# Packing eight row flags into one word and rolling a skipped path into a loop

## The chip, the cores and the metric

The kernel runs on one core of a Trainium2 chip. The metric is the device time of one execution, in microseconds (us); the profile adds the span from the core's first to its last instruction.

## The reference

Three layers follow each other on 3,072 tokens of 384 numbers:

- linear attention with a decaying state: `state = alpha * state + k v^T`, `y = q state`, for 4 batches of 8 heads;
- a dense layer: `h = x @ w_in`, `x = (h * cos(h)) @ w_out`, with 2,048 hidden numbers;
- a mixture of 8 experts: each token goes to the one expert with the greatest logit, and gets `gate * sigmoid * (relu(x @ w1[e]) @ w2[e])`, with 1,024 hidden numbers per expert.

Which expert a token goes to is known only on the chip, while the program runs.

## The kernel before

TensorE (PE) does the matrix products, most of them in three parts (high and low halves of both operands). Attention and the dense layer are staged in six groups of four units, with an order of work written out by hand over slots `J`. In each group the tokens are routed: `route_logits`, `route_rank` and `route_rows` work out the row of each token in a DRAM tensor `xs`, and `route_send` scatters the rows with four indirect DMAs issued by GpSimd (POOL). `xs` has a region of `REG` rows for each expert. `base` holds the next free row of each region, `ebase` its first row.

After the last group's dense layer the kernel goes over to the experts. The first 256 rows (`EARLY`) of expert 0 were sent by earlier groups, and `first(j)` and `second(j)` work on them while the last group is routed. Then `begin(0)` loads the other 192 rows of expert 0 (`load_rows`), `rows_trans` turns them on PE, and the loop over the eight experts runs: `e_stage1` for eight blocks of hidden numbers (two PSUM banks in turn, `banks[0]` and `banks[1]`), then the second product for each tile of rows, then `e_out`, which scales on ScalarE (ACT) and scatters the rows to `out` by an indirect DMA of POOL. `load_expert` loads the next expert's weights and splits them in halves in small steps, on SyncE's (SP) DMA queue, ACT and VectorE (DVE).

An expert's region has a fixed part of `CAP` = 448 rows. Where an expert has at most `LOW` = 384 rows, PE takes a shorter branch (`by_rows`, a branch on a register of PE, lines 649 to 657). The eight flags for it are worked out on DVE as a row of eight words, `fewi`, and PE loads them into eight registers just ahead of the loop (line 1031). Just before the loop three banks are set to zero (line 1037), and PE's first product of the loop writes the first of them.

Rows beyond `CAP` go through a general path after the loop. All engines load one word, the largest count of extra tiles (`nov`, line 1088), and branch over the path when it is zero (line 1089); with these inputs it is zero. The path is written out eight times, one copy for each expert, each with a loop over tiles inside. Line 1216 is the program's end. In the stretch of the loop the order on PE, ACT, DVE and SP is that of the code (`manual_schedule`); POOL's order, and the code after the loop, are placed by the scheduler.

Of the kernel before, what the change touches and what calls it, by code (L numbers as in the profile page):

```python
# [8 lines left out]
F32 = mybir.dt.float32  # L9
F32R = mybir.dt.float32r  # L10
BF16 = mybir.dt.bfloat16
U32 = mybir.dt.uint32
I32 = mybir.dt.int32
ACTF = mybir.ActivationFunctionType
ALU = mybir.AluOpType
AX = mybir.AxisListType
PSUM = bass.MemoryType.PSUM
ENG = mybir.EngineType
# [10 lines left out]
E = 8  # L29
# [5 lines left out]
CAP = 448  # L35
LOW = 384
NOV = -(-(NT - CAP) // 128)
REG = CAP + 128 * NOV
# [12 lines left out]
CEB = CW8 + GU * E  # L51
CTOK = CEB + E
CROW = CTOK + NU
CCOL = CROW + 1


@with_exitstack
def kernel(
# [11 lines left out]
    nc = tc.nc  # L70
# [38 lines left out]
    base = const.tile([128, E], F32, name="base")  # L109
# [415 lines left out]
    def route_rows(g):  # L525
        oh, rp = rk.pop(g)
        t = s_p.tile([128, GU, E], F32, tag="rk", name="rk")
        nc.vector.tensor_tensor(
            out=t, in0=rp[:, 0], in1=base.rearrange("p (o e) -> p o e", o=1).to_broadcast([128, GU, E]), op=ALU.add
        )  # L530
        nc.vector.tensor_tensor(out=t, in0=t, in1=oh, op=ALU.mult)
        pf = s_p.tile([128, GU, 1], F32, tag="pf", name="pf")
        nc.vector.tensor_reduce(out=pf, in_=t, axis=AX.X, op=ALU.add)
        pu = s_p.tile([128, GU, 1], U32, tag="pu", name="pu")
        nc.vector.tensor_copy(pu, pf)
        nc.vector.tensor_tensor(out=base, in0=base, in1=rp[:, 1, 0], op=ALU.add)
        if g == NG - 2:

            nc.vector.tensor_scalar_max(base[:, 0:1], base[:, 0:1], float(EARLY))
        rk[g] = pu  # L540
# [404 lines left out]
    with tc.manual_schedule(engines={ENG.PE, ENG.Activation, ENG.DVE, ENG.SP}):  # L945
# [7 lines left out]
        def second(j):  # L953
            for t in range(n_t):
                e_part2(early, t, accs[t], j)
# [22 lines left out]
            x1_rows(g, s)  # L978
        route_rank(g)
        route_rows(g)  # L980
        for s in range(GU):
            route_send(g, s)
        second(1)
# [7 lines left out]
        second(5)  # L991
        first(7)
        second(6)
        m1.close()

        m2 = ExitStack()
# [5 lines left out]
        def begin(e):  # L1002
            r0 = EARLY if e == 0 else 0
            return load_rows(e, r0, CAP - r0, z_p, "xe")
# [4 lines left out]
        for t in range(n_t):  # L1009
# [2 lines left out]


        nt = o_p.tile([128, E + 1], F32, name="nt")
        few = o_p.tile([128, E], F32, name="few", bufs=1)
        fewi = o_p.tile([128, E], U32, name="fewi", bufs=1)
        nc.vector.tensor_tensor(out=nt[:, 0:E], in0=base, in1=ebase, op=ALU.subtract)
        nc.vector.tensor_scalar(
            out=nt[:, 0:E], in0=nt[:, 0:E], scalar1=float(127 - CAP), scalar2=127.0, op0=ALU.add, op1=ALU.max
        )  # L1020
        nc.vector.tensor_reduce(out=nt[:, E:E + 1], in_=nt[:, 0:E], axis=AX.X, op=ALU.max)

        nc.vector.tensor_scalar(
            out=few, in0=base, scalar1=float(LOW), scalar2=None, op0=ALU.subtract
        )
        nc.vector.tensor_tensor(out=few, in0=few, in1=ebase, op=ALU.is_le)
        nc.vector.tensor_copy(ntl, nt)
        nc.vector.tensor_scalar(out=ntl, in0=ntl, scalar1=7, scalar2=None, op0=ALU.logical_shift_right)

        nc.vector.tensor_copy(fewi, few)  # L1030
        few_r = nc.values_load_multi_w_load_instructions(fewi[0:1, 0:E], engines=[ENG.PE], min_val=0, max_val=1)[1]


        banks = [ps_h.tile([128, 512], F32, tag="h", name="hp") for _ in range(2)]
# [2 lines left out]
            nc.vector.memset(b, 0.0)  # L1037

        for e in range(E):
            r["few"], r["banks"] = few_r[e], banks  # L1040
            steps = load_expert(e + 1, vr_p if e % 2 else vl_p) if nxt else []

            def step():
                if steps:
                    for f in steps.pop(0):
                        f()

            hbs = []
            for j in range(NEF):

                n = r["n"]
                hb = h_p.tile([128, 2 * n], F32R, tag="hb", name="hb")
                e_stage1(r, j, hb[:, 0:n], [(slice(0, n - 64), hb[:, n + 64:]), (slice(n - 64, n), hb[:, n:n + 64])])
                hbs.append(hb)
                if j % 2:
                    step()
            r["gates"] = gates(z_p, r["xe"][:, :, DM:], len(r["tiles"]))
            n_t = len(r["tiles"])
            for i, t in enumerate((n_t - 1, *range(n_t - 1))):
                if i == n_t // 2 and nxt:  # L1060
                    rows_trans(nxt, z_p, "exh", "exl")
                step()
                if i == n_t - 1:
                    while steps:
                        step()
                ot = o_p.tile([128, DM], F32, tag="ot", name="ot")
                if r["tiles"][t] == 64:
                    op = e_acc(r, t, i, 128)
                    for m in by_rows(r.get("few"), (1, 0)):
                        if m:  # L1070
                            for j in range(NEF):
                                e_part2_both(r, t, op, j, hbs[j])
                    low = o_p.tile([64, DM], F32, tag="low", name="low", bufs=1)
                    nc.scalar.copy(low, op[64:128])
                    nc.vector.tensor_tensor(out=low, in0=op[0:64], in1=low, op=ALU.add)
                    op = low
                else:
                    op = e_acc(r, t, i)
                    for j in range(NEF):
                        e_part2(r, t, op, j)  # L1080
                e_out(r, t, op, ot)
            r = nxt
            nxt = begin(e + 2) if e + 2 < E else None
    m2.close()
    at2.close()


    nov = nc.values_load(ntl[0:1, E:E + 1], min_val=0, max_val=NOV)
    with tc.If(nov > 0):
        with tc.tile_pool(name="ov_p", bufs=1, side="left") as ov_p:  # L1090
            f1 = ov_p.tile([128, KD, EF], F32, name="f1")
            f2 = ov_p.tile([128, NEF, DM], F32, name="f2")
            rid = ov_p.tile([128, 1], F32, name="rid")
            lim = ov_p.tile([128, 1], F32, name="lim")
            far = ov_p.tile([128, 1], F32, name="far")
            ri = ov_p.tile([128, 1], U32, name="ri")
# [4 lines left out]
            oo = ov_p.tile([128, DM], F32, name="oo")  # L1101
            nc.vector.memset(zo, 0.0)
            nc.vector.memset(zo[:, ROW - 1:ROW], float(NT))
            for e in range(E):
                nc.sync.dma_start(out=f1, in_=w1[e].rearrange("(k p) f -> p k f", p=128))
                nc.sync.dma_start(out=f2, in_=w2[e].rearrange("(k p) f -> p k f", p=128))
                r0 = e * REG + CAP
                nc.vector.tensor_scalar_add(rid, c_sb[:, CROW:CROW + 1], float(r0))
                nc.vector.tensor_copy(lim, base[:, e:e + 1])
                n_e = nc.values_load(ntl[0:1, e:e + 1], min_val=0, max_val=NOV)  # L1110
                with tc.For_i(0, n_e, 1) as it:

                    nc.vector.tensor_tensor(out=far, in0=rid, in1=lim, op=ALU.is_lt)
                    nc.vector.scalar_tensor_tensor(
# [5 lines left out]
                        out=xs, out_offset=bass.IndirectOffsetOnAxis(ap=ri, axis=0),  # L1120
                        in_=zo, in_offset=None, bounds_check=E * REG - 1, oob_is_err=False,
                    )
                    nc.sync.dma_start(out=xo[:, 0, :], in_=xs[bass.ds(it * 128 + r0, 128), :])
                    gt, tk = gates(ov_p, xo[:, :, DM:], 1)
                    tp = ps_m.tile([128, KD, C], F32, tag="m", name="tp")
                    for k in range(KD):
# [28 lines left out]
def _layout(inputs):  # L1155
# [32 lines left out]
    for n in range(NU):  # L1188
        c[:, CTOK + n] = (n % B) * S + (n // B) * C + perm
    c[:, CROW] = np.arange(128)  # L1190
    return {
        "units": u.reshape(NU, 128, UCOL),
        "cst": c,
# [26 lines left out]
```

## Time and profile before

| | |
|---|---|
| device time, median of 3 runs | 814.5 us (813.9 to 815.12) |
| device time of the profiled execution | 812.32 us |
| its span | 810.5 us |
| mean granted TensorE clock | 0.981 |
| PE busy | 769.4 us (95%) |
| DVE busy | 501.9 us (62%) |
| ACT busy | 425.3 us (52%) |
| POOL busy | 316.6 us (39%) |

The device time of the profiled execution holds the span and 1.8 us around it. Busy times are those of instructions that do work: register loads, branches and semaphore instructions are not in them, and have rows of their own under the engine's name with a q (POOLq, PEldq).

### The profile page before, as it was taken

The page shows a single profiled execution, that of the slowest core. Times are in us where ns is not written, and L with a number is a line of the kernel's source. Part 1 is how long each engine was busy: PE and PEld are TensorE (multiplying, and loading weights), DVE is VectorE, ACT ScalarE, POOL GpSimd, SP SyncE. Part 2 cuts the span into 40 slices and gives each one's busy share as a digit, 9 for nine tenths or more (in the row PEclk, how much of TensorE's full clock was granted, in tenths as well). Part 3 has the DMA queues.
Part 4 walks back from the last instruction along what each step waited for, and adds up shares of the span by engine and source line. Part 5 has one row for each costly group of instructions (what it writes and reads, how often), then busy time and mean ns, then how long its engine had stood idle before and what let it go on. Part 6 is the DMA issues. An engine that isn't in the chain of part 4 may idle for free.

```text
span 810.5 us, 13963 instructions
## 1 busy us (share of the span) xinstructions
PE 769.4 (95%) x5346; PEld 655.7 (81%) x5346; DVE 501.9 (62%) x955; ACT 425.3 (52%) x782; POOL 316.6 (39%) x304
## 2 busy tenths in 40 slices
PE   8679899999999999999999999999699999999994
PEld 5557777888888888888888888889699999999994
DVE  8999998675467537663676334744565655655530
ACT  2454565754575457644665467555354545554420
POOL 3566756544355335543464424662011101101101
PEclk9998999999999999999999999999899999999998
DMA  9524452713201230113010101211565445645201
GB/s 326 205 94 159 170 199 100 243 60 112 80 1 54 73 125 1 54 59 109 31 55 20 41 0 59 89 50 44 182 192 181 135 142 176 191 123 159 67 13 34
DMA packets 46881, 85.31 MB, mean 105 GB/s; under 512 B 4152, under 2 KB 38488, under 8 KB 44240
## 3 DMA queue, kind: packets, MB, share of 16 engines
q1 hardware_dynamic: 43344, 74.67, 28.1%
q0 software_dynamic: 3456, 9.57, 3.2%
q8 instruction: 50, 0.82, 0.4%
q14 instruction: 31, 0.25, 0.1%
HBM read 69.01 MB, written 15.99 MB: 105 GB/s over the span
## 4 chain that ended last, share of the span: by engine, by line
PE 52%; issue 27%; DVE 11%; POOL 4%; DMA 2%; ACT 1%; POOLq 0%; SPq 0%; ACTq 0%; DVEq 0%
PE acc L418 22%; PE hp L379 21%; POOL out_dram L711 4%; DVE cv L347 3%; PE sc L211 2%; DMA un<-in_units_dram 2%; DVE cv L352 2%; PE yp L269 2%; PE yp L261 2%; DVE cv L356 2%; PE pp L285 1%; PE tp L442 1%; DVE t L397 1%; DVE t L392 1%; DVE w L151 1%
## 5 line engine op out<-in xcount | busy, mean ns | idle before, releaser
L405 POOL TENSOR_TENSOR gl<-t,gh 128x512 fp32r<-128x512 f32 x95 | 127.8, 1345 | 182.2 <-ACT gh L404 152.5
L386 ACT ACTIVATE t<-hp 128x512 f32<-128x512 f32 x96 | 57.3, 596 | 140.1 <-PE hp L379 130.4
L397 DVE TENSOR_TENSOR t<-hp,t 128x512 f32<-128x512 f32 x96 | 65.7, 684 | 89.3 <-ACT t L394 89.3
L392 DVE SCALAR_TENSOR_TENSOR t<-t,hp 128x512 f32<-128x512 f32 x96 | 65.7, 684 | 79.7 <-ACT t L386 79.6
L711 POOL DMA_INDIRECT out_dram<-ot,tk x32 | 31.3, 979 | 205.9 <-ACT ot L710 205.6
L687 PE MATMUL op<-h,hb 128*128 128x384 f32 x384 | 102.4, 338 | 1.7 <-PEq L654 1.7
L418 PE MATMUL acc<-gh,woh 128*128 128x512 f32 x288 | 90.3, 421 | 0.0
L677 DVE SCALAR_TENSOR_TENSOR hb<-hp,hb 128x64 fp32r<-128x64 f32 (+3 forms) x136 | 45.3, 372 | 70.1 <-ACT hb L675 70.0
L379 PE MATMUL hp<-xh,wih 128*128 128x512 f32 x288 | 83.6, 398 | 3.7 <-DVE t L397 3.1
L418 PE MATMUL acc<-gl,woh 128*128 128x512 f32 x288 | 84.2, 399 | 0.0
L418 PE MATMUL acc<-gh,wol 128*128 128x512 f32 x288 | 83.9, 399 | 0.0
L379 PE MATMUL hp<-xh,wil 128*128 128x512 f32 x288 | 82.6, 395 | 0.0
L379 PE MATMUL hp<-xl,wih 128*128 128x512 f32 x288 | 82.5, 395 | 0.0
L393 ACT ACTIVATE t<-t 128x512 f32<-128x512 f32 x96 | 60.7, 632 | 38.3 <-DVE t L392 38.3
L675 ACT ACTIVATE hb<-hp 128x448 fp32r<-128x448 f32 (+2 forms) x72 | 36.3, 504 | 72.3 <-PE hp L671 70.3
L599 DVE TENSOR_TENSOR l<-raw,h 128x768 fp32r<-128x768 f32 x60 | 57.3, 957 | 25.8 <-ACT h L595 25.0
L687 PEld LDWEIGHTS op<-h,hb 128*128 128x128 f32 x384 | 69.7, 188 | 3.0 <-issue 3.0
L394 ACT ACTIVATE t<-t,halfpi 128x512 f32<-128x512 f32 x96 | 69.6, 725 | 3.1
L379 PEld LDWEIGHTS hp<-xh,wih 128*128 128x128 f32 x288 | 54.4, 191 | 18.0 <-DVE t L397 2.2
L418 PEld LDWEIGHTS acc<-gh,wol 128*128 128x128 f32 x288 | 55.1, 191 | 13.4
L418 PEld LDWEIGHTS acc<-gl,woh 128*128 128x128 f32 x288 | 54.9, 191 | 12.8
L379 PEld LDWEIGHTS hp<-xl,wih 128*128 128x128 f32 x288 | 54.5, 189 | 12.9
(144 smaller groups left out, 1454.4 us busy)
## 6 DMA issues: line engine op xcount, KB each, us to landing
raw<-in_w_dram SPq DMA_DIRECT2D x64, 384.0 KB, 3.4
un<-in_units_dram SPq DMA_DIRECT2D x20, 1032.0 KB, 4.9
raw<-in_w_in_dram SPq DMA_DIRECT2D x16, 384.0 KB, 3.7
raw<-in_w_out_dram SPq DMA_DIRECT2D x16, 384.0 KB, 4.1
xs<-zrow SPq DMA_DIRECT2D x8, 591.0 KB, 5.8
xe<-xs SPq DMA_DIRECT2D x7, 591.0 KB, 5.1
un<-in_units_dram SPq DMA_DIRECT2D x4, 512.0 KB, 6.2
un<-in_units_dram SPq DMA_DIRECT2D x4, 256.0 KB, 6.8
```

The source lines that it names most:

```text
L379: nc.tensor.matmul(out=hp, lhsT=w[:, k, fs], rhs=x[:, k, :], start=(n == 0), stop=(n == 3 * KD - 1))
L386: nc.scalar.activation(out=t, in_=hps[g, j], func=ACTF.Copy, bias=MAGIC)
L392: nc.vector.scalar_tensor_tensor(out=t, in0=t, scalar=MAGIC, in1=hp, op0=ALU.subtract, op1=ALU.subtract)
L393: nc.scalar.activation(out=t, in_=t, func=ACTF.Abs)
L394: nc.scalar.activation(out=t, in_=t, func=ACTF.Sin, scale=-TWO_PI, bias=halfpi)
L397: nc.vector.tensor_tensor(out=t, in0=hps.pop((g, j)), in1=t, op=ALU.mult)
L405: eng.tensor_tensor(out=gl, in0=gf, in1=gh.bitcast(F32), op=ALU.subtract)
L418: nc.tensor.matmul(out=acc[g][k], lhsT=w[:, j, ks], rhs=a, start=(j == 0 and n == 0), stop=(j == NF - 1 and n == 2),)
L599: (nc.vector.tensor_tensor if i < 4 else sub)(out=lo, in0=raws[i], in1=h.bitcast(F32), op=ALU.subtract)
L677: nc.vector.scalar_tensor_tensor(out=out_, in0=hp[:, c], scalar=0.0, in1=hh[:, c].bitcast(F32), op0=ALU.max, op1=ALU.subtract)
L687: nc.tensor.matmul(out=op, lhsT=a[:, sl], rhs=w[:, j, :], start=(j == 0 and i == 0), stop=(j == NEF - 1 and i == 2))
L711: sent = nc.gpsimd.indirect_dma_start(out=out, out_offset=bass.IndirectOffsetOnAxis(ap=tk[0:n, t, :], axis=0), in_=ot[0:n], in_offset=None ...
```

## The change

- The constants get 16 more columns, of which eight hold the powers of two.
- Right after `route_rows` of the last group, DVE works out the eight flags, multiplies them by the powers of two, adds them up and casts the sum to one word, `fews`. The three DVE instructions that made `fewi` go.
- PE loads that one word after `second(6)`, and takes each expert's flag out of it by a shift and a mask at the head of that expert's turn.
- `nov` is loaded by all engines at the end of the turn of expert 6 and no longer after the loop.
- The general path is one loop over the experts with the loop over tiles inside, and so stands in the program once.

```diff
 CROW = CTOK + NU
-CCOL = CROW + 1
+CPW = CROW + 1
+CCOL = CPW + 16
...
         route_rank(g)
         route_rows(g)
+
+        cnt = s_p.tile([128, E], F32, tag="rk", name="cnt")
+        nc.vector.tensor_tensor(out=cnt, in0=base, in1=ebase, op=ALU.subtract)
+        nc.vector.scalar_tensor_tensor(
+            out=cnt, in0=cnt, scalar=float(LOW), in1=c_sb[:, CPW:CPW + E], op0=ALU.is_le, op1=ALU.mult
+        )
+        bits = s_p.tile([128, 1], F32, tag="pf", name="bits")
+        nc.vector.tensor_reduce(out=bits, in_=cnt, axis=AX.X, op=ALU.add)
+        fews = s_p.tile([128, 1], U32, tag="pu", name="fews")
+        nc.vector.tensor_copy(fews, bits)
         for s in range(GU):
             route_send(g, s)
         second(1)
...
         first(7)
         second(6)
+        few = nc.values_load(fews[0:1, 0:1], engines=[ENG.PE], min_val=0, max_val=(1 << E) - 1)
         m1.close()
...
         nt = o_p.tile([128, E + 1], F32, name="nt")
-        few = o_p.tile([128, E], F32, name="few", bufs=1)
-        fewi = o_p.tile([128, E], U32, name="fewi", bufs=1)
...
-        nc.vector.tensor_scalar(
-            out=few, in0=base, scalar1=float(LOW), scalar2=None, op0=ALU.subtract
-        )
-        nc.vector.tensor_tensor(out=few, in0=few, in1=ebase, op=ALU.is_le)
         nc.vector.tensor_copy(ntl, nt)
         nc.vector.tensor_scalar(out=ntl, in0=ntl, scalar1=7, scalar2=None, op0=ALU.logical_shift_right)
-
-        nc.vector.tensor_copy(fewi, few)
-        few_r = nc.values_load_multi_w_load_instructions(fewi[0:1, 0:E], engines=[ENG.PE], min_val=0, max_val=1)[1]
...
         for e in range(E):
-            r["few"], r["banks"] = few_r[e], banks
+            r["few"], r["banks"] = nc.tensor.snap((few >> e) & 1), banks
...
             r = nxt
             nxt = begin(e + 2) if e + 2 < E else None
+            if e == E - 2:
+                nov = nc.values_load(ntl[0:1, E:E + 1], min_val=0, max_val=NOV)
...
-    nov = nc.values_load(ntl[0:1, E:E + 1], min_val=0, max_val=NOV)
-    with tc.If(nov > 0):
+    with tc.If(nov > 0, label="ov"):
...
-            for e in range(E):
-                nc.sync.dma_start(out=f1, in_=w1[e].rearrange("(k p) f -> p k f", p=128))
-                nc.sync.dma_start(out=f2, in_=w2[e].rearrange("(k p) f -> p k f", p=128))
-                r0 = e * REG + CAP
-                nc.vector.tensor_scalar_add(rid, c_sb[:, CROW:CROW + 1], float(r0))
-                nc.vector.tensor_copy(lim, base[:, e:e + 1])
-                n_e = nc.values_load(ntl[0:1, e:e + 1], min_val=0, max_val=NOV)
-                with tc.For_i(0, n_e, 1) as it:
+            nc.vector.tensor_scalar_add(rs, c_sb[:, CROW:CROW + 1], float(CAP))
+            nc.vector.tensor_copy(ends_, base)
+
+            with tc.For_i(0, E, 1) as e:
+                nc.sync.dma_start(out=f1, in_=w1[bass.ds(e, 1)].rearrange("o (k p) f -> p (o k) f", p=128))
+                nc.sync.dma_start(out=f2, in_=w2[bass.ds(e, 1)].rearrange("o (k p) f -> p (o k) f", p=128))
+                nc.vector.tensor_copy(rid, rs)
+                nc.vector.tensor_scalar_add(rs, rs, float(REG))
+                nc.vector.tensor_copy(lim, ends_[:, 0:1])
+                nc.vector.tensor_copy(next_, ends_)
+                nc.vector.tensor_copy(ends_[:, 0:E - 1], next_[:, 1:E])
+                with tc.For_i(0, nov, 1) as it:
...
-                    nc.sync.dma_start(out=xo[:, 0, :], in_=xs[bass.ds(it * 128 + r0, 128), :])
+                    nc.sync.dma_start(out=xo[:, 0, :], in_=xs[bass.ds(it * 128 + e * REG + CAP, 128), :])
```

## Rows read from the trace of the kernel before

**Rows 1.** Stretches: busy us (count) of PE, PEld, DVE, ACT, POOL; granted clock; DMA share; GB/s.

```profile
570.71:576.10 5.39, 0.00 (x0) 0.03 (x1) 2.93 (x12) 0.61 (x2) 1.99 (x2) 0.91 0.98 308
576.10:581.94 5.84, 5.84 (x27) 5.84 (x28) 1.44 (x5) 1.38 (x3) 0.00 (x0) 0.50 0.17 66
581.95:588.00 6.05, 5.68 (x48) 5.44 (x48) 4.20 (x13) 3.14 (x8) 0.00 (x0) 1.00 0.42 130
```

**Rows 2.** Line 1031, PE's load of the flags: ns min/median/max, first and last start.

```profile
L1031 PEldq FUSED_REGOPS  x8: 146/146/160, 573.4 to 575.4; - x8
...
L1031 PEldq TENSOR_LOAD <-fewi x1: 788/788/788, 572.5 to 572.5; - x1
```

**Rows 3.** DVE in order of time, ahead of the expert loop: start us, busy us.

```profile
571.40 0.16 DVE L1021 TENSOR_REDUCE nt<-nt 128x1 f32<-128x8 f32 x1
571.48 0.16 DVE L1023 TENSOR_SCALAR few<-base 128x8 f32<-128x8 f32 x1
...
571.76 0.30 DVE L1027 CAST ntl<-nt 128x9 uint32<-128x9 f32 x1
572.09 0.17 DVE L1028 TENSOR_SCALAR ntl<-ntl 128x9 uint32<-128x9 uint32 x1
572.17 0.16 DVE L1030 CAST fewi<-few 128x8 uint32<-128x8 f32 x1
572.44 1.03 DVE L1037 MEMSET hp<- 128x512 f32 x2
```

**Rows 4.** PE and POOL in order of time, the last work of each.

```profile
798.85 0.34 PE L687 MATMUL op<-h,hb 128*128 128x384 f32 x1
...
800.13 0.98 POOL L711 DMA_INDIRECT out_dram<-ot,tk  x1 [3.18 <-ACT ot L710]
```

**Rows 5.** Line 1088, the load of the count, on PE and POOL.

```profile
L1088 PEldq TENSOR_LOAD <-ntl x1: 332/332/332, 795.9 to 795.9; - x1
...
L1088 POOLq TENSOR_LOAD <-ntl x1: 484/484/484, 799.9 to 799.9; - x1
```

**Rows 6.** Line 1089, the branch over the general path, on POOL.

```profile
L1089 POOLq EVENT_SEMAPHORE  x5: 17/43/43, 803.3 to 803.7; - x5
...
L1089 POOLq COMPARE_BRANCH  x1: 53/53/53, 800.4 to 800.4; - x1
...
L1089 POOLq INC_SWDGE_SEM  x1: 1286/1286/1286, 803.8 to 803.8; - x1
```

**Rows 7.** Line 1216, the program's end, on POOL.

```profile
L1216 POOLq DRAIN  x3: 40/107/4647, 805.1 to 810.3; - x3
```

**Rows 8.** PE in order of time, first product of expert 0.

```profile
583.10 0.55 PE L671 MATMUL hp<-exh,h 128*128 128x192 f32 x3
...
584.15 0.51 PE L671 MATMUL hp<-exh,h 128*128 128x192 f32 x3
```

**Rows 9.** Stretches around two earlier stalls of PE, columns as in rows 1.

```profile
88.99:90.42 1.43, 0.00 (x0) 0.02 (x1) 1.39 (x5) 1.43 (x4) 1.22 (x2) 1.00 0.30 53
90.46:93.87 3.41, 3.41 (x17) 2.83 (x18) 3.41 (x7) 1.74 (x4) 3.03 (x4) 1.00 1.03 397
135.16:136.95 1.79, 0.00 (x0) 0.00 (x0) 1.70 (x3) 0.62 (x2) 0.03 (x1) 1.00 0.00 0
138.26:141.65 3.39, 3.39 (x10) 2.61 (x9) 2.09 (x4) 2.31 (x5) 2.70 (x6) 0.50 0.66 210
```

**Rows 10.** One of PE's waits from 540 us on: total, times, longest.

```profile
PE hp L671 <- ACT hb L675: 0.4, 1, 0.4
```

**Rows 11.** DVE's first work after the last group's routing.

```profile
561.20 0.42 DVE L677 SCALAR_TENSOR_TENSOR hb<-hp,hb 128x256 fp32r<-128x256 f32 x1 [2.79 <-ACT hb L675]
```

**Rows 12.** Line 654, the branches on the flags, on PE.

```profile
L654 PEldq COMPARE_BRANCH  x108: 65/174/337, 575.7 to 781.8; - x108
```

**Rows 13.** DMA issues: count, KB each, us from issue to landing.

```profile
c_sb<-in_cst_dram SPq DMA_DIRECT2D x1, 160.5 KB, 4.4
```

**Rows 14.** Line 711 from 799.9 us: the last scatter, from issue to landing.

```profile
DMA to landing us min/median/max: 3.0/3.0/3.0
```

More of the change, by code (lines that the diff above doesn't have):

```diff
@@ L1093 @@
             rid = ov_p.tile([128, 1], F32, name="rid")
+            rs = ov_p.tile([128, 1], F32, name="rs")
+            ends_ = ov_p.tile([128, E], F32, name="ends_")
+            next_ = ov_p.tile([128, E], F32, name="next_")
             lim = ov_p.tile([128, 1], F32, name="lim")
@@ L1190, in _layout @@
     c[:, CROW] = np.arange(128)
+    c[:, CPW:CPW + E] = 2.0 ** np.arange(E)
     return {
```

## Prediction

> **What bounds the kernel now.** I read the busy shares first, then the stretches where PE is idle, then what ended each idle time, and last the records of line numbers that do no work of their own (loads of registers, branches), because the change is made of those. PE bounds nearly everything: once expert 0 is running it does 5.68 of 6.05 us [rows 1], and every other engine has slack beside it. A change to the other engines is worth only what it gives PE, or what it takes from the tail after PE's last product. Two places have such time.
>
> [...] In the idle time stand PE's load of the flags, 0.79 us at 572.5, and eight register operations from 573.4 to 575.4 [rows 2]. They can't begin before the flags' cast on DVE ends at 572.17 + 0.16 = 572.33 [rows 3].
>
> The second is the tail. PE's last product ends at 798.85 + 0.34 = 799.19 [rows 4], and the span ends at 810.5: 11.3 us in which POOL sends the last scatter [rows 4], loads the count [rows 5], takes the branch over the general path [rows 6] and drains [rows 7].
>
> **The stall ahead of the loop.** With the flags already in a register, the loads and register operations leave the gap. PE then waits for the next late thing: the zeroing of the first bank. Two memsets took 1.03 us from 572.44 [rows 3], 0.515 each, so the first bank is ready at 572.95 now. The three DVE instructions for `fewi` stood in front of it. Without them the cast to `ntl` follows the reduce, at the 0.20 us that dependent small instructions need here, at 571.60 instead of 571.76; the shift comes 0.33 later, as now, at 571.93; it takes 0.17, and with a gap of some 0.08 the memset starts at 572.18, 0.26 earlier. The bank is zero at 572.7, and with 0.1 us for the signal PE starts at 572.8. It starts at 576.10 now: **-3.3 us**. The stall is 2.1 us, no longer 5.4.
>
> **The half clock after it.** PE did 27 products in 5.84 us at 0.50 [rows 1]. At full clock nine take 584.15 - 583.10 = 1.05 us [rows 8], so 27 take 3.15: the half clock costs 2.7 us. Does a stall of 2.1 us still lead to it? One of 1.79 us at 135.16 was followed by 3.39 us at 0.50; one of 1.43 us at 88.99 was followed by full clock [rows 9]. 2.1 us is on the far side of both, so I take a half-clock stretch again, but a short one, 3.4 us as in that row rather than 5.8. By the same rates it costs 3.4 x (1 - 1.05/1.95) = 1.6 us. The difference is **-1.1 us**. The ends: nothing gained, if the stretch is as long as before, and 2.7 - 0.4 = 2.3 gained if there is none, where 0.4 is one more wait of the kind in [rows 10], the bank's eviction behind the split of the next weights, which the half clock hides now.
>
> All PE time saved here reaches the end, since PE has no other idle time of that size behind it, and expert 1's rows and weights are first needed when the whole of expert 0 is done.
>
> **What is added there.** Four small DVE instructions after `route_rows`, about 0.2 us apart by [rows 3]: 0.8 us. DVE is idle for 2.79 us right there [rows 11], so they cost nothing as long as POOL's four row scatters, which stand behind them in the code, wait only for the row numbers made before them. If they waited for the flags too, everything up to the loop would be 0.8 later. PE's load of one word is issued behind `second(6)`. The load of the count shows how that goes: it ran on PE's queue at 795.9 while products went on until 799.19 [rows 4, 5], so the queue is read 3.3 us ahead and a load of 0.33 to 0.79 us [rows 2, 5] hides in that. Its ends are 0 and 0.8; I take 0, by the nearer row, which is the same kind of load in the same position behind products. A shift and a mask for each expert are one or two register operations of 0.15 us [rows 2] ahead of that expert's first branch. The 108 branches of 0.07 to 0.34 us already hide in the lead [rows 12]; I take 0, the upper end is 8 x 0.3 = 2.4. The first block of constants grows by 16 columns of 128 rows, 8 KB on 160.5 KB with a landing time of 4.4 us [rows 13]: at most 0.2, taken as 0. The loads of `nov` on SP, DVE, ACT and PE move under expert 7's products, where each has slack of microseconds: 0.
>
> **The tail.** POOL's load of the count, 0.48 us at 799.9, goes, so its branch stands at 799.9 and not at 800.4 [rows 5, 6]. What then? The branch itself took 0.05 us, but POOL's next instruction came at 803.3: 2.85 us with nothing [rows 6]. The short branches of line 654, over some twenty instructions, take 0.07 to 0.34 us in all [rows 12]. So the distance matters, and now one copy of the path is jumped over instead of eight; I take the wait as gone. [...]
>
> Next is a wait for the scatters. The branch not taken raises the counters of the DMAs that the path would have issued. Today the path holds sixteen scatters in its eight copies, spread over all the scatter counters, so POOL waits for each of them, the last scatter's too, before it raises them (1.29 us at 803.8 [rows 6]). With two scatters in the one copy it should wait for fewer and older ones. The last scatter lands at 800.13 + 3.0 = 803.1 [rows 4, 14]; if POOL must still wait for it, only 0.5 us of the tail can go. If not, POOL's next limit is its own work on that scatter, until 801.1 [rows 4]. Then 1.29 us for the counters, a drain of 4.65 us [rows 7] and the same last 0.8 us give 801.1 + 1.29 + 4.65 + 0.8 = 807.9 instead of 810.5: **-2.6 us**. The ends are 0, if the drain waits for something that does not move, and 2.6.
>
> **Sum.** -3.3 - 1.1 - 2.6 = -7.0. The profiled execution took 812.3 us (its span and 1.8 around it), so the like execution would take 805.3. The median of the runs is 814.5, 2.2 above it; I carry the difference over: **807.5**.
>
> **The rivals.** (a) The tail moves little: the branch still waits 2.85 us, or POOL still waits for the last scatter, or the drain ends where it did. Then 0.5 us of it goes: 814.5 - 3.3 - 1.1 - 0.5 = 809.6. For it: the landing at 803.1 is only 0.7 us before the counters are raised. Against it: two scatters in the path instead of sixteen. (b) No half clock, with the tail as forecast: 814.5 - 3.3 - 2.3 - 2.6 = 806.3. For it: the full clock after 1.43 us; against: the half clock after 1.79. (c) One of the hidden pieces isn't hidden, the scatters wait for the flags or PE's load stands bare, and the tail gives 0.5: 809.6 + 0.8 = 810.4, or 811.5 with half the per-expert register work bare. (d) Slower: PE's load of `nov` behind expert 6 stops PE as the load of line 1031 does now, because it waits for DVE with nothing queued. Its price is the whole of today's stall, 5.4 + 2.7 = 8.1 us, and it decides from 7.0: 815.6. For it, PE's stall at 1031 is such a load; against it, the same word's load ran ahead of PE without a wait. (e) The change does nothing that counts: PE's gain is eaten by expert 1's weights and the tail stays, 814.5 or less by under 1.6. Nothing in the rows speaks for it.
>
> **How the numbers follow.** Forecast 0.42, (a) 0.30, (b) 0.14, (c) 0.08, (d) 0.04, (e) 0.02. The range reaches from a little under (b), with the tail and clock terms a little better than taken, to between (c)'s two values: 805.5 to 811.0. It holds the forecast, (a), (b) and half of (c). About 0.2% (1.6 us) can be told from no change here. Faster by more: all but (d), (e) and the bad edge of (c), 0.93; the same 0.03; slower 0.04.
>
> **What would show it.** Right: PE idle near 2 us before expert 0's first product, ended by the memset; no group of register operations in it; at most some 3.4 us at 0.50 after it; four DVE rows near 558.5 in idle time; POOL's first instruction after the branch within some 0.2 us of it, and the span ending less than 9 us after PE's last product. Wrong: a gap of PE at an expert's start, POOL's scatters of rows starting 0.8 us later, a wait of near 3 us behind POOL's branch, or a drain that is longer by as much as it starts earlier.

## The result, and the profile after

The changed kernel takes **805.39 us** (median of 4 runs, 803.29 to 807.06), the kernel before 814.71 us on the same chip (813.9 to 815.12): 9.3 us less, a ratio of 0.9886 with a 95% interval of 0.986 to 0.9911. The forecast was 807.5 us, a gain of 7.0, and its range ended at 805.5, 0.1 us above the result. The direction and the two places named were right; the size was too small, and a third place was missing. The profiled execution of the changed kernel took 805.95 us, its span 804.2.

The sections of the execution can be laid side by side, with the borders read as PE's starts and ends, in us:

| | before | after | difference | forecast |
|---|---|---|---|---|
| from the start to PE's last product ahead of the stall | 570.70 | 572.40 | +1.70 | 0 |
| PE's stall ahead of expert 0 | 5.40 | 2.32 | -3.1 | -3.3 |
| expert 0 | 19.93 | 18.80 | -1.1 | -1.1 |
| experts 1 to 7 | 203.15 | 202.10 | -1.05 | 0 |
| from PE's last product to the end | 11.35 | 8.57 | -2.8 | -2.6 |

These sum to -6.3, and the two profiled executions differ by 6.4 (812.32 and 805.95). I don't put the first line down to the change: up to there the work is the same but for the flags and the longer constants, and stretches of half clock fall differently from one execution to the next (mean granted clock from 26 to 144 us: 0.93 before, 0.90 after). In the profiles of the experiments below PE reached that point at 571.72 to 572.44 us without the flags' edit and at 571.02 to 572.95 with it; some tenths of a microsecond of cost can't be excluded by that. Without that line the change gains 8.0.

**The stall.** Stretches of the changed kernel, to set against [rows 1]; columns as there.

```profile
572.40:574.70 2.30, 0.00 (x0) 0.02 (x1) 1.99 (x8) 0.61 (x2) 1.62 (x2) 1.00 0.97 254
...
576.24:579.66 3.42, 3.42 (x19) 3.42 (x18) 1.80 (x5) 1.50 (x4) 0.00 (x0) 0.50 0.65 241
579.66:585.50 5.84, 5.47 (x46) 5.22 (x46) 3.85 (x12) 2.89 (x8) 0.00 (x0) 1.00 0.49 135
```

PE idles for 2.3 us in place of 5.4, and 3.42 us at 0.50 follow in place of 5.84. What ends the idle time stands in PE's waits from 572 us on:

```profile
PE hp L672 <- DVE hp L1039: 2.3, 1, 2.3
```

That is the zeroing of the first bank, as forecast, and DVE in order of time shows how it comes so late, beside [rows 3]:

```profile
573.32 0.45 DVE L1032 CAST ntl<-nt 128x9 uint32<-128x9 f32 x1
573.80 0.17 DVE L1033 TENSOR_SCALAR ntl<-ntl 128x9 uint32<-128x9 uint32 x1
574.08 1.02 DVE L1039 MEMSET hp<- 128x512 f32 x2
```

The three instructions for `fewi` are gone from between them. The cast takes 0.45 us here and 0.30 in [rows 3], which is most of the 0.2 us by which the stall is longer than the 2.1 forecast.

**The flags.** They are worked out on DVE right behind the last group's rows, first and last of the four:

```profile
559.90 0.17 DVE L984 TENSOR_TENSOR cnt<-base,c_sb 128x8 f32<-128x8 f32 x1
...
560.50 0.15 DVE L991 CAST fews<-bits 128x1 uint32<-128x1 f32 x1
```

Line 1005 is PE's load of the word, and line 655 the branches on its bits:

```profile
L1005 PEldq TENSOR_LOAD <-fews x1: 484/484/484, 567.4 to 567.4; - x1
L1005 PEldq FUSED_REGOPS  x1: 165/165/165, 568.0 to 568.0; - x1
```

```profile
L655 PEldq ALU_OP  x135: 36/36/42, 570.7 to 778.3; - x135
L655 PEldq COMPARE_BRANCH  x108: 67/174/345, 570.8 to 778.4; - x108
```

The load stands 5 us ahead of PE's stall and stops nothing. The shifts and masks came out as 135 register operations of 36 ns ahead of the 108 branches, more in number than the one or two for each expert that the prediction expected and shorter than its 0.15 us. PE waited on those branches in four places, 0.5 us at the longest and 1.8 us in all; before, by the same view of the waits, it was 0.4 us and 1.7 us, in four places too.

The view of POOL's waits names the flags as what the first scatter of rows waited for. Before and after:

```profile
559.12 0.99 POOL L544 DMA_INDIRECT xs<-xr,pu  x1 [6.50 <-DVE base L536]
```

```profile
560.58 0.99 POOL L545 DMA_INDIRECT xs<-xr,pu  x1 [6.51 <-DVE bits L989]
```

But the scatter starts as long behind the start of the sum into `base`, the last instruction of `route_rows`, as it did: 559.12 - 558.26 = 0.86 us before, 560.58 - 559.71 = 0.87 after, and 0.84 to 0.87 in the other eleven profiles. So the flags don't hold it up.

**The tail.** Loads of the count (line 1087), POOL's last scatter, the branch (line 1092) and POOL's drain (line 1227), beside [rows 4 to 7]:

```profile
L1087 PEldq TENSOR_LOAD <-ntl x1: 316/316/316, 762.5 to 762.5; - x1
...
L1087 POOLq TENSOR_LOAD <-ntl x1: 493/493/493, 796.3 to 796.3; - x1
```

```profile
796.56 0.98 POOL L712 DMA_INDIRECT out_dram<-ot,tk  x1 [3.18 <-ACTq L1092]
```

```profile
L1092 PEldq COMPARE_BRANCH  x1: 320/320/320, 792.4 to 792.4; - x1
...
L1092 POOLq COMPARE_BRANCH  x1: 45/45/45, 796.9 to 796.9; - x1
L1092 POOLq EVENT_SEMAPHORE  x1: 17/17/17, 797.4 to 797.4; - x1
L1092 POOLq INC_SWDGE_SEM  x1: 1278/1278/1278, 797.4 to 797.4; - x1
```

```profile
L1227 POOLq DRAIN  x3: 45/107/4638, 798.7 to 803.9; - x3
```

POOL's load of the count did not move: it still stands behind the last scatter's issue. But the next instruction after the branch comes 0.4 us later in place of 2.85, one wait of 17 ns stands there in place of five, and the raising of the counters (`INC_SWDGE_SEM`) starts at 797.4, before POOL's own work on the last scatter ends at 796.56 + 0.98 = 797.54 and before its landing at 796.56 + 2.8 = 799.4. In the records of the two traces the five waits and the raising name the semaphores of the last eight scatters, 111 to 118, the last one's (118) among them; the one wait and the raising in the changed kernel name 112 and 111 alone, those of the first two of the eight. The drain is as long as before and starts earlier. Counted from PE's end, the time behind the branch gives 2.4 us and the waits ahead of the counters 0.35; the rest of the tail is as long as before.

Is that time the jump, or a wait for the last scatter, which landed at 803.1, just ahead of POOL's next instruction at 803.3? DVE, whose branch comes 12 us before that scatter is issued, settles it. Before and after:

```profile
L1089 DVEq EVENT_SEMAPHORE  x2: 21/21/21, 790.8 to 790.9; - x2
...
L1089 DVEq COMPARE_BRANCH  x1: 63/63/63, 787.9 to 787.9; - x1
```

```profile
L1092 DVEq COMPARE_BRANCH  x1: 63/63/63, 783.7 to 783.7; - x1
L1092 DVEq EVENT_SEMAPHORE  x1: 21/21/21, 784.3 to 784.3; - x1
```

It too lost 2.8 us before and 0.5 after, with that scatter not yet issued. So the time goes with the length of the jump. The DMA queues of the kernel before, from POOL's branch to its next instruction (800.4 to 803.3 us), show packets of the kind `instruction` (count, MB, share of 16 engines):

```profile
q8 instruction: 1, 0.02, 2.2%
q14 instruction: 2, 0.02, 1.9%
```

The same view of the kernel after, from 796.9 to 797.4, has none. That these packets make the 2.85 us, or a part of it, isn't shown by this.

**Experts 1 to 7.** Stretches of the changed kernel, experts 1 and 6 and 7, and then the same three of the kernel before:

```profile
593.51:624.78 31.27, 31.27 (x174) 30.05 (x174) 18.24 (x37) 14.81 (x27) 4.25 (x4) 1.00 0.58 176
...
734.61:765.61 31.00, 31.00 (x173) 30.07 (x173) 15.96 (x33) 14.52 (x26) 3.87 (x4) 1.00 0.27 82
765.61:795.61 30.00, 30.00 (x161) 28.62 (x160) 6.84 (x22) 7.42 (x15) 3.87 (x4) 1.00 0.07 23
```

```profile
596.03:627.49 31.46, 31.46 (x174) 30.07 (x174) 18.27 (x37) 14.84 (x27) 4.25 (x4) 1.00 0.55 173
...
737.41:768.89 31.48, 31.48 (x174) 30.09 (x174) 15.94 (x33) 14.52 (x26) 3.87 (x4) 1.00 0.26 80
768.89:799.18 30.29, 30.29 (x161) 28.62 (x160) 6.83 (x22) 7.42 (x15) 3.87 (x4) 1.00 0.07 24
```

PE is busy without a gap at full clock in both, and does the same products; yet these three, the experts with more than 384 rows, are shorter by 0.2, 0.5 and 0.3 us. PE in order of time shows it, two rows of three products each in the first block of expert 6, before and after:

```profile
739.26 0.78 PE L671 MATMUL hp<-exh,h 128*128 128x448 f32 x3
739.88 0.78 PE L671 MATMUL hp<-exl,h 128*128 128x448 f32 x3
```

```profile
734.61 0.76 PE L672 MATMUL hp<-exh,h 128*128 128x448 f32 x3
735.21 0.76 PE L672 MATMUL hp<-exl,h 128*128 128x448 f32 x3
```

Three products of 448 columns are spaced 0.62 us apart before, 206.7 ns each, and 0.60 after, 200.0 ns each. In expert 7 it is 206.7 before and 202.7 after, and in the first five blocks of expert 1 too, while its last three are at 206.7 or just below. No step of the prediction has this.

### The profile page after: what moved, and what is told of

Its sections match the earlier page's. It is cut to its first block, busy times and chain, and to the rows that moved or that the text cites. A ratio compares the mean times of both kernels' runs of the same rounds, so it can differ in the third digit from the quotient of the medians.

```text
span 804.2 us, 14074 instructions
## 1 busy us (share of the span) xinstructions
PE 770.3 (96%) x5346; PEld 656.6 (82%) x5346; DVE 502.8 (63%) x956; ACT 425.2 (53%) x782; POOL 315.1 (39%) x304
## 4 chain that ended last, share of the span: by engine, by line
PE 53%; issue 26%; DVE 11%; POOL 4%; ACT 1%; POOLq 0%; ACTq 0%; DVEq 0%
PE acc L419 22%; PE hp L380 21%; POOL out_dram L712 4%; DVE cv L348 3%; PE sc L212 2%; DVE cv L353 2%; PE yp L270 2%; PE yp L262 2%; DVE cv L357 1%; PE pp L286 1%; PE tp L443 1%; DVE w L152 1%; DVE t L398 1%; DVE t L393 1%; PE lp L475 1%
## 5 line engine op out<-in xcount | busy, mean ns | idle before, releaser
L380 PEld LDWEIGHTS hp<-xh,wih 128*128 128x128 f32 x288 | 54.8, 192 | 18.3 <-DVE t L398 2.2
```

Source lines behind the costliest of these rows:

```text
L380: nc.tensor.matmul(out=hp, lhsT=w[:, k, fs], rhs=x[:, k, :], start=(n == 0), stop=(n == 3 * KD - 1))
```

## The experiments

The theory: the gain is the loads leaving PE's stall, the shorter jump with its one wait, and the spacing of products, which follows from where tiles lie in memory. The rivals: the tail's gain comes from the early load of the count; the spacing comes from the flags' instructions; the rest of the stall and the half clock are not the memset's.

| kernel | median us (lowest to highest, runs) | before, same chip | ratio, 95% interval |
|---|---|---|---|
| e1_flags | 808.74 (807.28 to 809.81, 6) | 813.18 | 0.9944, 0.9928 to 0.9959 |
| e2_tail | 810.02 (809.91 to 810.45, 6) | 813.18 | 0.9957, 0.9943 to 0.9971 |
| e3_copies | 808.02 (806.07 to 810.25, 6) | 813.18 | 0.9935, 0.9914 to 0.9956 |
| e4_after | 805.55 (804.85 to 806.75, 5) | 813.18 | 0.9906, 0.9889 to 0.9922 |
| e5_pad | 813.35 (811.32 to 814.31, 12) | 814.04 | 0.9993, 0.9983 to 1.0003 |
| e6_banks | 801.9 (801.46 to 803.12, 5) | 814.04 | 0.9853, 0.9839 to 0.9867 |
| e7_nopath | 804.06 (802.58 to 805.35, 4) | 814.04 | 0.9878, 0.9859 to 0.9896 |
| e8_poolload | 802.07 (800.99 to 802.83, 5) | 814.04 | 0.9853, 0.9839 to 0.9867 |
| e10_place | 812.74 (812.1 to 814.21, 10) | 813.75 | 0.9989, 0.998 to 0.9999 |
| e9_opad | 808.31 (1 run) | 813.75 | none from a single run |
| e11_pad2 | 805.75 (1 run) | 813.75 | none from a single run |

**The two halves of the change.** e1_flags is the changed kernel with the old tail; e2_tail is the kernel before with the new tail; e4_after is the whole change again, beside them on one chip.

```diff
 e1_flags, against the kernel after
-            if e == E - 2:
-                nov = nc.values_load(ntl[0:1, E:E + 1], min_val=0, max_val=NOV)
...
-    with tc.If(nov > 0, label="ov"):
+    nov = nc.values_load(ntl[0:1, E:E + 1], min_val=0, max_val=NOV)
+    with tc.If(nov > 0):
...
-            with tc.For_i(0, E, 1) as e:
+            for e in range(E):
 e2_tail, against the kernel after
-CCOL = CPW + 16
+CCOL = CROW + 1
...
-        few = nc.values_load(fews[0:1, 0:1], engines=[ENG.PE], min_val=0, max_val=(1 << E) - 1)
...
+        few_r = nc.values_load_multi_w_load_instructions(fewi[0:1, 0:E], engines=[ENG.PE], min_val=0, max_val=1)[1]
...
-            r["few"], r["banks"] = nc.tensor.snap((few >> e) & 1), banks
+            r["few"], r["banks"] = few_r[e], banks
```

> The change with the flags' part alone: eight copies of the general path and the load of the count after the loop, as in the kernel before. Theory (two separate gains): PE's stall ahead of expert 0 falls from 5.4 to about 2.3 us and expert 0 is some 1.1 us shorter, the tail after PE's last product stays at 11.35 us, so 4.2 to 5.3 us less than before. Rival (the gain is mostly in the tail, and what PE saves is eaten later): under 2 us less. Rival on the products of 448 columns (their spacing fell from 206.7 to 200 to 203 ns with the change, 1.0 us over the experts 1 to 7): if the 64 bytes by which the larger block of constants moves every later tile did it, this kernel has the short spacing and the one with the tail alone has 206.7; if it differs from execution to execution, the two don't sort that way.

> The change with the tail's part alone: one copy of the general path in a loop, the count loaded at the end of expert 6, but the eight flags as eight words loaded ahead of the loop. Theory: PE's stall is 5.4 us and the half clock after it as before, the tail falls from 11.35 to about 8.6 us: 2.5 to 3 us less than before. Rival (the tail is bounded by the landing of the last scatter or by a drain that ends where it did): 0 to 0.6 us less. On the products of 448 columns: 206.7 ns if the place of the tiles sets their spacing, any of the values if it differs from execution to execution.

> The changed kernel once more, unaltered, beside the others on one chip. Theory: 8 to 9.5 us less than before, and e1's and e2's gains add up to that within 1 us. Where the sum of the two falls short by more, the two parts help each other. Its profile shows whether the spacing of the products of 448 columns (200 to 206.7 ns) and the places of the half-clock stretches ahead of 140 us repeat or differ from execution to execution.

e1 gains 813.18 - 808.74 = 4.4 us, e2 gains 3.2, together 7.6, and the whole change gains 813.18 - 805.55 = 7.6: the halves add up, though the whole was expected to gain 8 to 9.5. Each gain also sits where it should. In e1 the stall is 2.31 us, ended by the same memset, and the tail 11.26:

```profile
573.33 0.55 PE L672 MATMUL hp<-exh,h 128*128 128x192 f32 x3 [2.31 <-DVE hp L1039]
```

In e2 the stall is 5.85 us and the profile shows nothing that PE waited for ("issue"), as before; the tail is 8.58:

```profile
577.57 0.71 PE L671 MATMUL hp<-exh,h 128*128 128x192 f32 x2 [5.85 <-issue]
```

Experts 1 to 7 took 202.1 us in e1 and 203.2 in e2, with the old spacing: that gain belongs to the flags' half.

**Eight copies with the early load.** e3_copies is the changed kernel with the path written out eight times again, but the count loaded early.

```diff
-    with tc.If(nov > 0, label="ov"):
+    with tc.If(nov > 0):
...
-            with tc.For_i(0, E, 1) as e:
+            for e in range(E):
...
-                with tc.For_i(0, nov, 1) as it:
+                n_e = nc.values_load(ntl[0:1, e:e + 1], min_val=0, max_val=NOV)
+                with tc.For_i(0, n_e, 1) as it:
```

> The change, but the general path again as eight copies; the count is loaded at the end of expert 6 as in the change. Theory (the length of what is jumped over and its sixteen scatters make the tail): POOL's next instruction comes some 2.8 us after its branch and it waits for the last scatter, the tail is near 11 us again, 2.3 to 2.8 us more than the change. Rival (the early load of the count made the gain): the tail stays near 8.6 us, within 0.6 us of the change.

Its branch, line 1092:

```profile
L1092 POOLq EVENT_SEMAPHORE  x5: 17/43/43, 798.5 to 798.8; - x5
...
L1092 PEldq COMPARE_BRANCH  x1: 3442/3442/3442, 791.2 to 791.2; - x1
...
L1092 POOLq COMPARE_BRANCH  x1: 53/53/53, 795.8 to 795.8; - x1
L1092 POOLq INC_SWDGE_SEM  x1: 1286/1286/1286, 798.9 to 798.9; - x1
```

With eight copies POOL's next instruction is again 2.7 us behind the branch, five waits are back, and the tail is 11.19 us. It takes 808.02 - 805.55 = 2.5 us more than the change; the tails differ by 11.19 - 8.58 = 2.6. So the loop is nearly the whole of the tail's gain, and the load of the count, moved up as the change does it, is worth 11.26 - 11.19 = 0.07 us, the difference from e1's tail. On POOL that load stands behind the last scatter's issue in e3 too; what it is worth to move it there, e8 shows below. The last scatter had landed at 798.25, ahead of the first of the five waits, so its landing held nothing up; whether it would behind a short jump, no run shows. PE's branch record grows from 0.32 to 3.44 us as well, where nothing waits for it. For a path that is jumped over, the loop was the better of the two here: 805.55 us, against 808.02 with eight copies.

**Where the spacing comes from.** The change moves tiles: 16 more columns of constants are 64 bytes of each partition (one of a tile's 128 rows in on-chip memory), and the two flag tiles that it removes were 32 bytes each. Four kernels move tiles alone. e5_pad is the kernel before with 16 unused columns. e10_place is the kernel before with both of the change's shifts, the columns and the flag tiles laid into a buffer that exists already. e9_opad is the kernel after with two unused tiles in the place of the old flag tiles. e11_pad2 is the kernel after with 16 columns more.

```diff
 e5_pad, against the kernel before
-CCOL = CROW + 1
+CCOL = CROW + 17
 e10_place, against the kernel before
-CCOL = CROW + 1
+CCOL = CROW + 17
...
-        few = o_p.tile([128, E], F32, name="few", bufs=1)
-        fewi = o_p.tile([128, E], U32, name="fewi", bufs=1)
+        both = o_p.tile([128, DM], F32, tag="ot", name="both")
+        few, fewi = both[:, 0:E], both[:, E:2 * E].bitcast(U32)
 e9_opad, against the kernel after
+        o_p.tile([128, E], F32, name="few", bufs=1)
+        o_p.tile([128, E], U32, name="fewi", bufs=1)
 e11_pad2, against the kernel after
-CCOL = CPW + 16
+CCOL = CPW + 32
```

> The kernel before with nothing but 16 more columns, never read, in the block of constants, so that every later tile lies 64 bytes further on, as in the change. Theory (the place of the tiles sets the spacing of the products of 448 columns): spacing 200 to 203 ns in place of 206.7, experts 1 to 7 together 1.0 us shorter, stall 5.4 to 5.9 us and tail 11.35 us unaltered, so 0.6 to 1.4 us less than before. Rival (the flags' own instructions on PE's queue, a shift and a mask for each branch in place of registers that are ready, change the pace of the products): spacing 206.7 ns, no change of the time.

> The kernel after the change with two small unused tiles put back where the eight flags' tiles were, so that the tiles behind them lie 64 bytes further on; no other instruction. If the place of the tiles sets the spacing of the 448-column products, expert 7's go back from 202.7 to 206.7 ns (its stretch from 30.0 to about 30.3 us) and nothing else moves; if the flags' instructions set it, expert 7 stays at 202.7 ns.

> The kernel before the change with the tiles alone placed as the change places them: 16 unused columns in the counts' tile and the two flags' tiles put inside a buffer that exists already; every instruction stays. If the place sets the spacing, the 448-column products of experts 1, 6 and 7 are spaced 202.7, 200.0 and 202.7 ns, experts 1 to 7 take about 202.1 us in place of 203.15, the stall stays 5.4 to 6.0 us, the jump 2.8 us, and the time is about 1.0 us below the kernel before (ratio 0.9988). If the flags' instructions set it, expert 7 stays at 206.7 ns and the time falls by 0.4 us.

> The kernel after the change with 16 further unused columns in the counts' tile, so that every tile behind it lies another 64 bytes further on. If the place sets the spacing, some of the 448-column products of experts 1, 6 and 7 change theirs among 200.0, 202.7 and 206.7 ns, with experts 1 to 7 between 202 and 203.2 us; if not, all stay as after the change.

The spacing of the 448-column products, in ns, from PE's starts:

| kernel | expert 1, first block | expert 6 | expert 7 |
|---|---|---|---|
| before, e2_tail | 206.7 | 206.7 | 206.7 |
| e5_pad | 202.7 | 200.0 | 206.7 |
| e10_place | 202.7 | 200.0 | 202.7 |
| after, e1, e3, e4, e6, e7, e8 | 202.7 | 200.0 | 202.7 |
| e9_opad | 202.7 | 200.0 | 206.7 |
| e11_pad2 | 206.7 | 203 to 205 | 202.7 |

Experts 6 and 7 in e9, then in e10, as stretches:

```profile
736.57:767.68 31.11, 31.11 (x174) 30.17 (x173) 15.96 (x33) 14.51 (x26) 3.87 (x4) 1.00 0.26 81
```

```profile
767.68:797.97 30.29, 30.29 (x161) 28.62 (x160) 6.83 (x22) 7.42 (x15) 3.87 (x4) 1.00 0.06 23
```

```profile
738.77:769.77 31.00, 31.00 (x174) 30.07 (x173) 15.95 (x33) 14.50 (x26) 3.87 (x4) 1.00 0.27 82
769.77:799.77 30.00, 30.00 (x161) 28.62 (x160) 6.83 (x22) 7.42 (x15) 3.87 (x4) 1.00 0.07 24
```

e10 has every instruction of the kernel before and the spacing of the kernel after; its experts 1 to 7 take 201.9 us and its time falls by 1.0 us (0.9989, interval 0.998 to 0.9999). e9 has every instruction of the kernel after, and expert 7 goes back to 206.7 ns and 30.29 us (expert 6, expected to stay, takes 31.11 in place of 31.00 at the same 200.0 ns, so other products move a little too). The columns alone do only a part: in e5 expert 7 keeps 206.7 ns, experts 1 to 7 take 202.8 us, 0.4 less than before where 1.0 was expected, and the time (0.9993, interval 0.9983 to 1.0003) can't be told from the kernel before. So the place of the tiles sets the spacing, and the flags' instructions don't: that rival is out. The expectation of e11 that the spread would change again held; expert 6 took a value between the others. Its experts 1 and 6 cost 31.44 and 31.45 us, and experts 1 to 7 take 203.1 us, as in the kernel before: 64 bytes more took the gain back. Which tile's place counts, and why, stays open: all tiles behind the moved one shift together.

**The rest of the stall.** e6_banks is the kernel after with two banks zeroed ahead of the turning of the rows; e8_poolload is e6 with POOL's load of the count tied ahead of expert 7's scatters.

```diff
 e6_banks, against the kernel after
+        banks = [ps_h.tile([128, 512], F32, tag="h", name="hp") for _ in range(2)]
+        for b in banks:
+            nc.vector.memset(b, 0.0)
...
-        banks = [ps_h.tile([128, 512], F32, tag="h", name="hp") for _ in range(2)]
...
-        for b in banks[:3]:
-            nc.vector.memset(b, 0.0)
+        nc.vector.memset(banks[2], 0.0)
 e8_poolload, further
+        while first_loads:
+            tc.add_manual_dep(
+                sent.ins, first_loads.pop(),
...
-                nov = nc.values_load(ntl[0:1, E:E + 1], min_val=0, max_val=NOV)
+                loads, (nov,) = nc.values_load_multi_w_load_instructions(ntl[0:1, E:E + 1], min_val=0, max_val=NOV)
+                first_loads.extend(l.ins.name for l in loads if l.ins.engine == ENG.Pool)
```

> The change, and the first two banks are zeroed right after the rows of expert 0 are asked for, while DVE waits for them, and no longer behind the count. Theory (the rest of PE's stall is the zeroing, and the half clock after it comes from the stall): the stall falls from 2.3 us to 0.0 to 0.5 us, no half-clock stretch begins in expert 0, which takes 17.2 to 17.6 us in every profile; 2 to 4 us less than the change. Rival (the next late thing is close behind: PE then waits for the low halves of expert 0's rows): stall above 1 us, and 0 to 1.5 us less.

> As e6, and POOL's load of the count is tied ahead of the scatters of expert 7; the scheduler had left it behind the last of them. Theory (POOL's queue is the tail): the branch comes 0.5 us earlier and the tail falls from 8.57 to 8.0 to 8.3 us, so 0.3 to 0.5 us less than e6. Rival (the raising of the counters waits for POOL's work on the scatter anyway): the tail stays within 0.15 us.

PE in e6, the last product ahead of expert 0 and its first, and then its waits from 540 us on:

```profile
572.29 0.34 PE L688 MATMUL op<-h,hb 128*128 128x384 f32 x1
572.47 0.47 PE L672 MATMUL hp<-exh,h 128*128 128x192 f32 x3
```

```profile
PE hp L672 <- DVE hb L678: 0.8, 2, 0.6
...
PE tp L643 <- DVE hp L1021: 0.7, 1, 0.7
```

The stall is gone, the clock stays at 1.00 through expert 0, and two waits come up: 0.65 us ahead of the turning of the rows, where the kernel after waited as long for their DMA, and 0.63 ahead of expert 0's second block. Expert 0 takes 17.9 us for that, and 18.3 in e8, more than the 17.2 to 17.6 expected. The time is 801.9 us, 0.9853 of before, and its interval (0.9839 to 0.9867) lies below that of the change itself in e4 (0.9889 to 0.9922), each against the kernel before on its own chip. So the memset was the whole of the stall that was left. e8's tail is 8.01 us where e6's is 8.57, as its theory said, but its time, 802.07, can't be told from e6's. POOL's last scatter in e8, and the raising of the counters:

```profile
793.14 0.98 POOL L713 DMA_INDIRECT out_dram<-ot,tk  x1 [3.18 <-ACTq L1101]
```

```profile
L1101 POOLq INC_SWDGE_SEM  x1: 1283/1283/1283, 793.4 to 793.4; - x1
```

The counters are raised 0.7 us before POOL's work on the scatter ends, at 793.14 + 0.98 = 794.12: the tail doesn't wait for that work there, and the load of the count, 0.5 us, was in its way.

**No general path.** e7_nopath is the kernel after without the load of the count, the branch and the path; it leaves out the work on rows beyond 448 for an expert, of which these inputs have none.

```diff
-            if e == E - 2:
-                nov = nc.values_load(ntl[0:1, E:E + 1], min_val=0, max_val=NOV)
...
-    with tc.If(nov > 0, label="ov"):
...
```

> The change without the general path, its branch and the load of the count: surplus rows beyond 448 per expert are left out (there are none here). Theory (POOL's drain of 4.64 us is a fixed time from where it starts): without the load (0.49 us), the wait behind the branch (0.43) and the raising of counters (1.3), the drain begins when POOL's own work on the last scatter ends, some 1.3 us earlier, and the tail is 7.2 to 7.6 us. Rival (the drain ends at a time set by the last scatter): it becomes longer by what it starts earlier, the tail stays at 8.5 us.

POOL's last scatter, and the drain at the program's end:

```profile
795.79 0.98 POOL L712 DMA_INDIRECT out_dram<-ot,tk  x1 [3.18 <-ACT ot L711]
```

```profile
L1158 POOLq DRAIN  x3: 45/107/5865, 795.6 to 802.0; - x3
```

The tail is 7.38 us, as expected, but not for the reason given: the drain is no fixed time from its start. It starts early and lasts 5.87 us, until 801.4, which is 4.65 us after the scatter's end at 795.79 + 0.98 = 796.77. With the path it lasts 4.64 us after the counters are raised. So some 4.6 us stand behind POOL's last work with the path and without it, and the path still costs 8.57 - 7.38 = 1.2 us of tail, about the raising of the counters. In the medians that can't be told apart: e7's interval (0.9859 to 0.9896) overlaps that of the change in e4 (0.9889 to 0.9922).

## Why the prediction fell short

**The stall, forecast -3.3.** The mechanism was right: the loads left the gap, and the bank's zeroing ended it. The size was -3.1 between the two profiles. Over the four profiles with the old load (before, e2, e5, e10) the stall was 5.40 to 6.03 us, with the new one 2.31 or 2.32 in all seven (after, e1, e3, e4, e7, e9, e11), so that the typical gain is nearer 3.5.

**The half clock, forecast -1.1, ends 0 and -2.3.** A short half-clock stretch after a stall of 2.3 us is what the first profile shows, and it was not the rule. Expert 0 in the kernel after, in e4 and in e9, which do the same work there behind the same stall:

```profile
574.71:593.51 18.80, 18.43 (x124) 18.15 (x125) 12.57 (x34) 10.71 (x23) 1.28 (x2) 0.91 0.67 210
```

```profile
574.78:592.28 17.50, 17.07 (x124) 16.62 (x125) 12.50 (x34) 10.79 (x23) 1.28 (x2) 1.00 0.74 228
```

```profile
575.25:595.14 19.89, 19.89 (x125) 19.79 (x126) 12.69 (x34) 10.79 (x23) 1.28 (x2) 0.83 0.63 201
```

The clock's mean is 0.91, 1.00 and 0.83. It stayed full in e3, e4 and e11 (17.5 us), was half for 3.4 us in after, e1 and e7 (18.8), and for 6.8 us in e9 (19.9). With the long stall it was half for 6.8 us each time, and expert 0 took 19.17 to 19.93. The means, 18.4 over the seven and 19.5 over the four, are the forecast's 1.1 apart, but two executions with the same work behind the same stall lie 2.4 us apart (e9 and e3). That the first pair of profiles shows just the forecast's 1.1 is luck. A stretch of 3.4 us costs 18.80 - 17.50 = 1.3 us, where the prediction had 1.6. Rival (b) and the forecast are the same kernel in different executions.

**The tail, forecast -2.6.** Measured -2.8. The causes that were named are shown by e3: the jump and the waits come back with the eight copies, 2.3 us of the 2.6 by the jump and 0.4 by the five waits. The scatter's landing is no part of it. Two steps on the way to -2.6 were wrong. POOL's load of the count did not go: the scheduler left it behind the last scatter's issue, and e8, which moves it, has a tail 0.56 us shorter. And POOL's own work on the last scatter, the limit that the prediction had set, is none: the counters are raised 0.1 us before it ends in the kernel after and 0.7 before in e8. By that limit the prediction had the counters start 801.1 - 799.19 = 1.9 us behind PE's end; they start 1.8 us behind it, with the load and 0.4 us left of the jump ahead of them. That the two agree is luck. Rival (a) is out.

**What is added.** The four flag instructions, the load, the register work and the longer constants cost nothing that shows, as forecast, but for the tenths of a microsecond that the first line of the table leaves open. Rivals (c), (d) and (e) have no trace: the scatters don't wait for the flags, PE has no gap at an expert's start, and the load of line 1087 doesn't stop PE.

**The step that failed** is in the sum, -3.3 - 1.1 - 2.6: it has no term for experts 1 to 7, which it left as they were, since all that the change puts there hides behind PE. That holds, and yet PE's own products there became 1.05 us shorter, because the tiles moved (e10 and e9). With it the like sum is -3.1 - 1.1 - 1.05 - 2.8 = -8.0, and -9.3 where expert 0 keeps the full clock. The measured gains, 9.3 us (interval 7.3 to 11.4) on one chip and 7.6 (6.3 to 9.0) on the other, both hold -8.0; the forecast of 7.0 lies just outside the first and inside the second. What the first chip's 9.3 has beyond 8.0 the two profiles don't place.

**Carrying the 2.2 us over** from profile to median leaves the gain as it is, but it says that the two profiles don't stand alike to their medians: the profiled execution of before reached the stall at 570.70, the one after at 572.40, on equal work. After the change the profiled execution lies 0.6 us above its median.

## What to carry to other kernels

A load into registers that waited for its data stalled its engine for the whole chain behind it, 3.1 of PE's 5.4 us here; move such a load to where its data has long been made, and ask what was second in line, since removing that too (the zeroing, e6) took the time from 0.9906 of before to 0.9853. The skipped path cost by its length in the program, 2.3 us on POOL, and 0.4 by the waits ahead of the counters: keep such a path short, as a loop. Before a difference of 0.1% is given to an edit, move the tiles alone by as many bytes and time that.

## What was not expected of the hardware

- Products of the same shape on an undisturbed PE at full clock were spaced 200.0, 202.7 or 206.7 ns, by where tiles lie within a partition; shifts of 64 bytes changed it, up to 0.5 us for an expert of 31.5 us and about 1 us over experts 1 to 7.
- After one and the same stall of 2.31 us the granted clock was 1.00 throughout, or 0.50 for 3.4 us, or 0.50 for 6.8 us, in seven executions 3, 3 and 1 times.
- POOL's drain ended 4.6 us after POOL's last work, with the path and without it.
- A branch over eight copies of a skipped path kept POOL 2.7 to 2.9 us from its next instruction and DVE 2.8; over one copy it was 0.4 and 0.5.
